# Moving part of the second step additions from VectorE to GpSimd as int32 pair sums, with a new instruction order

## The chip, the cores and the metric

The kernel runs on one core of one Trainium2 chip. The metric is the device time of one execution in microseconds. Three runs of the kernel before gave 702.07, 702.99 and 703.46 us; the median is 702.99 us.

## The reference

Two attention blocks over the same input x (2048 positions, 512 features, 32 heads of 16), mixed by a gate for each position:

```python
g = _sigmoid((x * gate_w).sum(-1, keepdims=True))
# block A: softmax attention
scores = jnp.einsum("bhqd,bhkd->bhqk", q, k) * (Dh ** -0.5)
p = _softmax(scores, axis=-1)
o = jnp.einsum("bhqk,bhkd->bhqd", p, v)
a = o.transpose(0, 2, 1, 3).reshape(B, S, D) @ wo
# block B: linear attention
phi = lambda t: jnp.where(t > 0, t + 1, jnp.exp(t)) + 1e-6
kv = jnp.einsum("bhsd,bhse->bhde", phi(k), v)
num = jnp.einsum("bhqd,bhde->bhqe", phi(q), kv)
den = jnp.einsum("bhqd,bhd->bhq", phi(q), phi(k).sum(s))[..., None] + 1e-6
b = (num / den).transpose(0, 2, 1, 3).reshape(B, S, D) @ wo_B
return g * a + (1 - g) * b
```

Nearly all the work is the exponential of the scores of block A: 32 heads x 2048 x 2048 values.

## The kernel before, in words

**Rounds and units.** The scores are made in 32 rounds. A round is four heads (every second head of a group of eight) against 512 queries, and consists of 64 units; a unit is one head's 128 keys x 512 queries, one bank of PSUM. TensorE makes the scores of a unit (`ps<-Qpad,KT`), the exponential is taken, and TensorE multiplies the result with the values (`ps<-PT,Vaug` or `ps<-DP,Vaug`) into the accumulator of the round.

**Two ways to an exponential.** ScalarE takes the units in order, two or three banks with one ACTIVATE (line 1979, output tile PT). Beside it VectorE takes units from the back of the round: a "claim". Only units from number 40 up can be claimed (`4 * KB2`), so 24 of the 64 at most. For a claimed unit VectorE reads PSUM once (line 1518) and writes an int16 number whose bits, read as float16, are a coarse exponential. Four claimed units make a bundle (`NTRI = 4`, 2048 int16 numbers a partition). Then the same bundle is written twice more with 342 and with 683 added to each number (line 1566, the step additions, z = 1 and z = 2), and TensorE multiplies all three versions with values scaled by three weights; the weighted sum smooths out the coarse exponential. So a claimed unit takes three value products, a unit of ScalarE takes one.

**The order is planned.** All instructions are laid down when the kernel is built, by a planner that keeps an estimated clock for each engine. VectorE's work waits in a list (`items`) with priorities: 0 for claims made inside a ScalarE group and for accumulator copies, 1 for other evictions and side claims, 2 for checks, 3 for step additions. `pump` takes the best item that could start. `can_claim`, `claim_in_group` and `claim_beside` decide whether a further unit goes to VectorE: they ask `dve_load`, the VectorE work that is queued, against `RING_LOAD` (claims inside a group) or `CLAIM_LOAD` (others), and whether buffers are free (13 bundles, `NB`). `claim_round` gives the round of ScalarE (`act_round`) as long as 14 of its units are left, and the next round after that. Where nothing else is due, TensorE runs multiplications of the zero tile `warm` (`fill`).

**GpSimd in the kernel before.** After the start it only makes 12 products `OT<-oraw,rbc` (line 1246), planned with `POOL_TT = 1.3` us. While such an operation runs, `est_start` lets no VectorE operation that reads only SBUF start:

```python
if E is DV and not any(res in r_bank for res in reads):
    for a, b in pool_runs:
        if a <= t < b:
            t = b
```

A path that gives step additions to GpSimd exists (`EVERY`, `POOL_ADD`) and is switched off with `EVERY = 0`; there the addition is a `tensor_scalar` over 2048 int16 numbers, planned with 2.4 us.

Of the kernel before, what the change touches and what calls it, by code (L numbers as in the profile page):

```python
# [9 lines left out]
ALU = mybir.AluOpType  # L10
# [3 lines left out]
I32 = mybir.dt.int32  # L14
I16 = mybir.dt.int16
# [15 lines left out]
STEPS = (0, 342, 683)  # L31
NG4 = len(STEPS)
# [21 lines left out]
NTRI = 4  # L54
# [150 lines left out]
def d_sb(n, rate=1.0):  # L205
    return 0.15 + n * 1.042e-3 * rate
# [6 lines left out]
def bass_gated_mix__mha_block__linear_attn_block__prompt_kernel(  # L213
# [27 lines left out]
    pairs_ = [(t8, qc) for t8 in range(NT8 - 2) for qc in range(NQC)] + LAST_ORDER  # L241
    KV0, KV1 = 1.0, 1.2
    PRE_T = 5
    PRE_GAP = 8
    OUT_GAP = 8

    with ExitStack() as es:
        _cnt = [0]

        def SB(shape, dt, name):  # L250
            _cnt[0] += 1
            return es.enter_context(nc.sbuf_tensor(f"{name}_{_cnt[0]}", list(shape), dt))
# [48 lines left out]
        NTU = 512 * NTRI  # L301

        DP = SB([128, NB, NTU], BF16, "DP")
# [5 lines left out]
        rbc = SB([128, 512], FP32, "rbc")  # L309
        dev = SB([128, 2, 128], FP32, "dev")  # L310
        flag = SB([128, 1], I32, "flag")
        epool = SB([128, 2, 512], BF16, "epool")
        KVbd = SB([128, NCC, 128], BF16, "KVbd")
        Zsel = SB([128, NCC, 8], BF16, "Zsel")
# [35 lines left out]
        PE = _Eng("pe", SEM("s_pe"), ordered=True)  # L350
# [22 lines left out]
        R = _Res  # L373
# [20 lines left out]
        r_OT = [[R(f"OT{t}_{q}") for q in range(NQC)] for t in range(NT8)]  # L394
        r_rraw = [R(f"rraw{k}") for k in range(8)]
        r_dev, r_flag = R("dev"), R("flag")
        r_e = [R("e0"), R("e1")]
        r_phiK = [[R(f"phiK{s}_{k}") for k in range(4)] for s in range(2)]
        r_phi2 = [R(f"phi2{k}") for k in range(NTB // 2)]
# [16 lines left out]
        def est_start(E, reads, writes):  # L416
            t = E.t
            for res in list(reads) + list(writes):
                if res.we is not E:
                    t = max(t, res.tw + LAT)  # L420
                elif not E.ordered:
                    t = max(t, res.tw + SELF_T)
            for res in writes:
                t = max(t, res.tr + LAT)
# [8 lines left out]
        POOL_SOON = 0.3  # L433
        POOL_TT = 1.3
        POOL_V = 0.9
        POOL_ADD = 2.4
        EVERY = 0
        OT_POOL = 1
        V2_POOL = 0

# [16 lines left out]
        def blocked(it, reads, writes):  # L457
            return blocker(it, reads, writes) is not None
# [27 lines left out]
        def settle(reads, writes):  # L486
# [31 lines left out]
        def op(E, fn, reads=(), writes=(), dur=0.2, issue=None):  # L518
            settle(reads, writes)
            return _emit(E, fn, reads, writes, dur, issue)  # L520
# [11 lines left out]
                    res.pw += 1  # L532

        WAIT_BANK = 0.12

        def pump(now, look=0.25):
            try_close()
            while items and DV.t <= now + look:
                best = None
                for it in items:  # L540
                    o = it.ops[0]
                    if len(o) > 5 or blocked(it, o[1], o[2]):
                        continue
                    st = est_start(DV, o[1], o[2])
                    wait = st - DV.t
                    key = (wait > (WAIT_BANK if it.prio <= 1 else 0.12), it.prio, st, it.seq)
                    if best is None or key < best[0]:
                        best = (key, it, st)
                if best is None:
                    return  # L550
                if best[2] > now + look + WAIT_BANK:
                    return
                emit_item_op(best[1])

        def dve_load(now):
            return max(0.0, DV.t - now) + sum(o[3] for it in items for o in it.ops)
# [135 lines left out]
                                                   pattern=pattern, channel_multiplier=mult), reads=[w], writes=[w])  # L692

        op(PO, lambda: nc.gpsimd.memset(warm[:], 0.0), writes=[r_warm])  # L694
# [758 lines left out]


        tri = [None]
        closing = [None]
        z1_out = [None, None]
        ntri = [0]

        def claim_round():  # L1460
# [13 lines left out]
        def can_claim(now, js):  # L1474

            r = claim_round()
            if r is None:
                return None
            t8, qc, half = rounds[r]
            if (t8, qc, half) not in q_done or (t8, 3) not in k_ready:  # L1480
                return None
            u = next((u for u in range(NU - 1, 4 * KB2 - 1, -1) if u >= head[r] and u % 4 in js and u not in taken[r]), None)
            if u is None:
                return None
            kt, q, rd = unit_aps(r, u)
# [3 lines left out]
            if not try_close() and (tri[0] is None or len(tri[0][1]) == NTRI - 1):  # L1489
# [7 lines left out]
        def free_buffers():  # L1497

            used = [e[3] for e in pv_pending]
            held_ = [c[0] for c in (tri[0], closing[0]) if c is not None]  # L1500
# [25 lines left out]
            pv_pending.append((r, u, [(DP[:, i, 512 * k:512 * (k + 1)].bitcast(F16), z)], r_DP[i][k], Fraction(1, NG4)))  # L1526

        def close_tri():
            if tri[0] is not None and closing[0] is None:
                closing[0] = (*tri[0], [])  # L1530
                tri[0] = None
            try_close()

        def try_close():

            while closing[0] is not None:
                i, us, zs = closing[0]
                z = len(zs) + 1
                if z == NG4:
                    closing[0] = None  # L1540
                    return True
                free = free_buffers()
                if not free:
                    return False
                i2 = free[0]
                zs.append(i2)
                n = 512 * len(us)
                y = DP[:, i, 0:n].bitcast(I16)
                mine_, out_ = r_DP[i][0:len(us)], r_DP[i2][0:len(us)]
                if EVERY and z == NG4 - 1 and n == NTU and ntri[0] % EVERY == 0:  # L1550
                    push(3, [(lambda z=z, i2=i2, y=y, n=n: nc.gpsimd.tensor_scalar(
                        DP[:, i2, 0:n].bitcast(I16), y, 1.0, float(STEPS[z]), ALU.mult, ALU.add), mine_, out_, 0.0, None, POOL_ADD)])
                    if z1_out[0] is None:
                        pool_go([])
                    else:
                        z1_out[1] = out_
                else:
                    z1_out[:] = [out_, None]

                    def added(z=z, out_=out_):  # L1560
                        if z1_out[0] is out_:
                            z1_out[0] = None
                        if z == NG4 - 1 or z1_out[1] is not None:
                            z1_out[1] = None
                            pool_go(out_)
                    push(3, [(lambda z=z, i2=i2, y=y, n=n: nc.vector.tensor_single_scalar(DP[:, i2, 0:n].bitcast(I16), y, STEPS[z], ALU.add),  # L1566
                              mine_, out_, d_sb(n, 0.25), added)])
                for k, (r, u) in enumerate(us):
# [216 lines left out]
        RES_FROM = 60  # L1785
        MARGIN = 0.15
        PV_LAG = 14
        LATE = 9
        LAG_END = 12
        A_FIRST = 200  # L1790
        LATE_END = 0
# [225 lines left out]
            g += 1  # L2017


        while tri[0] is not None or closing[0] is not None:  # L2020
            close_tri()
            if closing[0] is not None and not pv_step(PE.t, force=True):
# [242 lines left out]
```

## Time and profile before

| | |
|---|---|
| Median of 3 runs | 702.99 us |
| The profiled execution, its own time | 702.72 us |
| Its span, first to last instruction | 701.0 us |
| ScalarE busy | 687.5 us, 98% |
| TensorE busy | 676.9 us, 97% |
| VectorE busy | 660.2 us, 94% |
| GpSimd busy | 24.1 us, 3% |
| Granted TensorE clock | 1.000 of full speed |

Busy times are unions: two operations of an engine that overlap count once. A group's mean is the duration of a single operation, which is longer than the distance from one start to the next where operations of an engine overlap at their ends. A row of a list of groups names the line, the engine, the operation, output and input, the count, and behind the bar the busy time, the mean in ns and the idle time in front with what ended it.

### The profile page before, as it was taken

The numbers are of one execution on the slowest core, as the hardware profiler recorded it, in microseconds if no ns is written. First come the engines' busy times: TensorE is split into PE (matmuls) and PEld (weight loads), VectorE is DVE, ScalarE is ACT, GpSimd is POOL, SyncE is SP. The second block draws the span as 40 slices with busy tenths as digits, with TensorE's granted clock in tenths as the row PEclk, the third lists the DMA queues.
The fourth block names the chain that finished last, engine by engine and source line by source line (L and its number), as shares of the span: only waits on it lengthen the run. The fifth ranks groups of instructions, "written<-read, shape, count | busy, mean of one in ns | idle before, by whom it ended". The sixth has DMA issues, their size and how long they took to land.

```text
span 701.0 us, 19208 instructions
## 1 busy us (share of the span) xinstructions
PE 676.9 (97%) x8181; PEld 205.6 (29%) x8181; DVE 660.2 (94%) x1140; ACT 687.5 (98%) x710; POOL 24.1 (3%) x31
## 2 busy tenths in 40 slices
PE   8999999999999999999999999999999999999997
PEld 4322223332223323232322232322222222222223
DVE  4599999999999998999999999999999998999995
ACT  6999999999999999999999999999999999999996
POOL 4000000000000000000000000000000000000000
PEclk9999999999999999999999999999999999999999
DMA  9800101000010001201010011101111201010101
GB/s 222 233 2 9 25 2 34 1 14 22 10 24 2 19 16 40 50 7 33 3 22 13 14 37 17 28 15 26 31 25 29 44 13 44 17 41 18 35 23 49
DMA packets 44815, 22.96 MB, mean 33 GB/s; under 512 B 33976, under 2 KB 40568, under 8 KB 44728
## 3 DMA queue, kind: packets, MB, share of 16 engines
q1 hardware_dynamic: 42712, 20.12, 12.7%
q10 hardware_dynamic: 2016, 1.57, 0.9%
q8 instruction: 67, 1.10, 0.7%
q14 instruction: 20, 0.16, 0.1%
HBM read 8.00 MB, written 2.10 MB: 14 GB/s over the span
## 4 chain that ended last, share of the span: by engine, by line
ACT 93%; PE 6%; DVE 1%; issue 0%; POOL 0%; ACTq 0%; POOLq 0%
ACT PT L1979 90%; PE ps L646 6%; ACT epool L929 2%; DVE DP L2075 0%; DVE xT L1847 0%; PE ps L653 0%; DVE KT L818 0%; DVE DP L2080 0%; DVE flag L2085 0%; POOL warm L694 0%; POOL dummy L663 0%; ACT eg L913 0%; ACTq L2188 0%; POOLq L2250 0%
## 5 line engine op out<-in xcount | busy, mean ns | idle before, releaser
L1979 ACT ACTIVATE PT<-ps 128x1024 bf16<-128x1024 f32 (+1 forms) x670 | 679.7, 1337 | 0.6 <-PE ps L646 0.5
L1518 DVE TENSOR_SCALAR DP<-ps 128x512 int16<-128x512 f32 x584 | 384.5, 683 | 13.4 <-PE ps L646 10.5
L646 PE MATMUL ps<-Qpad,KT 32*128 32x512 bf16 x2048 | 269.1, 384 | 17.6 <-ACT PT L1979 12.8
L1566 DVE TENSOR_SCALAR DP<-DP 128x2048 int16<-128x2048 int16 x292 | 193.8, 682 | 0.0
L646 PE MATMUL ps<-DP,Vaug 128*32 128x512 f16 x1741 | 188.1, 384 | 0.3 <-DVE oraw L1258 0.3
L646 PE MATMUL ps<-PT,Vaug 128*32 128x512 bf16 x1451 | 163.5, 385 | 0.6 <-DVE Vaug L873 0.5
L646 PEld LDWEIGHTS ps<-Qpad,KT 32*128 32x128 bf16 x2048 | 67.3, 91 | 289.1 <-ACT PT L1979 265.7
L646 PE MATMUL ps<-warm 128*32 128x512 bf16 (+1 forms) x510 | 72.8, 384 | 1.1 <-POOL warm L694 1.1
L646 PEld LDWEIGHTS ps<-DP,Vaug 128*32 128x32 bf16 x1741 | 46.4, 95 | 58.5 <-issue 34.0
L646 PEld LDWEIGHTS ps<-PT,Vaug 128*32 128x32 bf16 x1451 | 38.9, 94 | 52.4 <-issue 40.6
L1246 POOL TENSOR_TENSOR OT<-oraw,rbc 128x512 bf16<-128x512 f32 x12 | 15.6, 1303 | 524.5 <-DVE DP L1566 524.5
L646 PE MATMUL ps<-xT,wA 128*32 128x512 bf16 x432 | 32.1, 384 | 0.0
L929 ACT ACTIVATE epool<-ps 128x512 bf16<-128x512 f32 x32 | 27.4, 858 | 0.0
L646 PEld LDWEIGHTS ps<-warm 128*32 128x32 bf16 (+1 forms) x510 | 18.8, 97 | 19.8 <-issue 15.2
L1258 DVE COPY oraw<-ps 128x512 f32<-128x512 f32 x31 | 21.1, 682 | 0.1
L646 PE MATMUL ps<-wB,xT 128*32 128x512 bf16 x256 | 19.3, 384 | 0.0
L646 PE MATMUL ps<-xT,wB 128*32 128x512 bf16 x256 | 18.8, 383 | 0.0
L646 PE MATMUL ps<-woA,OT 128*32 128x512 bf16 (+1 forms) x226 | 18.6, 383 | 0.0
L934 DVE SCALAR_TENSOR_TENSOR phi<-ps,epool 128x512 bf16<-128x512 f32 x24 | 16.3, 680 | 0.0
L818 DVE CAST KT<-ps 128x512 bf16<-128x512 f32 (+1 forms) x16 | 10.7, 667 | 4.9 <-PE ps L646 4.9
L646 PE MATMUL ps<-wA,xT 128*128 128x128 bf16 x192 | 14.9, 220 | 0.0
L873 DVE CAST Vaug<-ps 128x512 bf16<-128x512 f32 x16 | 10.9, 683 | 2.3 <-PE ps L646 2.3
(104 smaller groups left out, 233.1 us busy)
## 6 DMA issues: line engine op xcount, KB each, us to landing
rbc<-oraw SPq DMA_DIRECT2D x16, 256.0 KB
OT<-in_A_x_dram SPq DMA_DIRECT2D x4, 512.0 KB, 7.2
Qpad<-Qs SPq DMA_DIRECT2D x124, 16.0 KB, 1.8
oraw<-oraw SPq DMA_DIRECT2D x60, 32.0 KB, 2.0
wA<-in_A_wqkv_dram SPq DMA_DIRECT2D x1, 1536.0 KB, 7.8
wB<-in_B_wqkv_dram SPq DMA_DIRECT2D x1, 1536.0 KB, 9.0
out_dram<-outt SPq DMA_DIRECT2D x12, 128.0 KB, 1.8
phi<-in_A_x_dram ACTq DMA_DIRECT2D x3, 256.0 KB, 6.1
```

The lines of the kernel that those rows point to most:

```text
L646: return lambda: nc.tensor.matmul(o, lhsT=l, rhs=r, start=start, stop=stop, skip_group_check=sg)
L818: push(1, [(lambda: nc.vector.tensor_copy(KT[:, par, c0:c1], src), [r_bank[b]], [r_KT[par][t]], d_psum(n), None)])
L873: ops = [(lambda: nc.vector.tensor_copy(v_group(NQC * par + v)[:, :, :, 0:16], src), [r_bank[b]], [r_V[par][v]], d_psum(512), lambda: v_do ...
L929: op(AC, lambda: nc.scalar.activation(epool[:, s, :], bank_ap(b), ACT.Exp), reads=[r_bank[b]], writes=[r_e[s]], dur=0.6, issue=0.48)
L934: (lambda: nc.vector.scalar_tensor_tensor(out=dst, in0=bank_ap(b), scalar=0.0, in1=epool[:, s, :], op0=ALU.max, op1=ALU.add), [r_bank[b], ...
L1246: push(1, [(lambda: (nc.gpsimd if on_pool else nc.vector).tensor_tensor(OT[:, t8, 512 * qc:512 * (qc + 1)], oraw[:, 0, :], rbc[:], ALU.mul ...
L1258: push(0, [(lambda: nc.vector.tensor_copy(oraw[:, half, :], acc), [r_acc], [r_oraw[half]], d_psum(512), evicted)])
L1518: push(0 if in_group else 1, [(lambda: nc.vector.tensor_scalar(DP[:, i, 512 * k:512 * (k + 1)].bitcast(I16), bank_ap(b), FRAC - Y_BIAS4, Y ...
L1566: push(3, [(lambda z=z, i2=i2, y=y, n=n: nc.vector.tensor_single_scalar(DP[:, i2, 0:n].bitcast(I16), y, STEPS[z], ALU.add), mine_, out_, d ...
L1979: op(AC, lambda p0=p0, b0=b0, n=n: nc.scalar.activation(PT[:, 512 * p0:512 * p0 + n], ps[:, 512 * b0:512 * b0 + n], ACT.Exp, scale=LN2 / F ...
```

## The change

On GpSimd the second step addition (z = 2) of every second bundle is now a `tensor_tensor` addition over 1024 int32 numbers: each holds two int16 numbers, and the other operand is one int32 number a partition (683 in both halves), read again and again. It is allowed only for a full bundle whose four units are of one round, where that round is the one that ScalarE works on and not the last. `POOL_ADD`, the planned length, is 1.97 us. `pool_go` is now asked at each step of the planner; a GpSimd addition goes out behind a VectorE step addition, and if a VectorE step addition could run and none has just run, that one is first put ahead of all other VectorE work (`boost`). Closed bundles form a queue in place of a single slot, and the additions of a bundle of a later round wait while another addition is listed. Some limits of the planner have new values, and the whole order is laid down anew. The diff, cut to its core:

```diff
-    PRE_GAP = 8
+    PRE_GAP = 6
...
+        step2 = SB([128, 2], I16, "step")
...
-        POOL_ADD = 2.4
-        EVERY = 0
+        POOL_ADD = 1.97
+        EVERY = 2
+        POOL_LEFT = 22
...
-        def pool_go(sync):
+        def pool_go(sync=None):
             for it in sorted(items, key=lambda i: i.seq):
                 o = it.ops[0]
                 if len(o) > 5 and not blocked(it, o[1], o[2]) and est_start(PO, o[1], o[2]) <= DV.t + POOL_SOON:
+                    if not last_add[1] and any(x.prio == 3 and len(x.ops[0]) == 5 and not blocked(x, x.ops[0][1], x.ops[0][2])
+                                               for x in items):
+                        boost[0] = True
+                        return
+                    boost[0] = last_add[1] = False
                     STATS["pool"] = STATS.get("pool", 0) + 1
-                    emit_item_op(it, sync)
+                    emit_item_op(it, last_add[0])
                     return
...
         def pump(now, look=0.25):
             try_close()
+            pool_go()
...
-                    key = (wait > (WAIT_BANK if it.prio <= 1 else 0.12), it.prio, st, it.seq)
+                    key = (wait > (WAIT_BANK if it.prio <= 1 else 0.12), -1 if it.prio == 3 and (boost[0] or (RUSH and it.ops[0][5:] == () and due_now(it))) else it.prio, st, it.seq)
...
                 emit_item_op(best[1])
+                pool_go()
...
+        op(PO, lambda: nc.gpsimd.memset(step2[:], STEPS[2]), writes=[r_step], dur=0.1)
...
-        GATE_AT = 4.5
+        GATE_AT = 3.5
...
-        PT_URGENT = 11
+        PT_URGENT = 12
...
-            if tri[0] is None and len(free_buffers()) < CLAIM_FREE:
+            if tri[0] is None and len(free_buffers()) < (CLAIM_FREE_OPEN if closing else CLAIM_FREE):
...
+                if len(free) < (LAZY if early else 1):
+                    return False
+                if not zs and sum(1 for it in items if it.prio == 3) >= (1 if early else MOST_ADDS):
                     return False
...
-                if EVERY and z == NG4 - 1 and n == NTU and ntri[0] % EVERY == 0:
-                    push(3, [(lambda z=z, i2=i2, y=y, n=n: nc.gpsimd.tensor_scalar(
-                        DP[:, i2, 0:n].bitcast(I16), y, 1.0, float(STEPS[z]), ALU.mult, ALU.add), mine_, out_, 0.0, None, POOL_ADD)])
...
+                if (EVERY and z == NG4 - 1 and n == NTU and ntri[0] % EVERY == 0 and us[0][0] == us[-1][0] < NR - 1
+                        and us[0][0] == act_round[0] and NU - len(taken[us[0][0]]) > POOL_LEFT):
+                    push(3, [(lambda z=z, i2=i2, y=DP[:, i, 0:n].bitcast(I32), n=n: nc.gpsimd.tensor_tensor(
+                        DP[:, i2, 0:n].bitcast(I32), y, step2[:].bitcast(I32).to_broadcast([128, n // 2]), ALU.add),
+                        mine_ + [r_step], out_, 0.0, None, POOL_ADD)])
...
-        Q_OFF = 0
+        Q_OFF = -4
...
-        CLAIM_LOAD = 3.3
-        LATE_CLAIM = 4.0
-        STARVE = 7
-        MAC_LOW = 0.47
+        CLAIM_LOAD = 3.7
+        LATE_CLAIM = 4
+        STARVE = 6.0
+        MAC_LOW = 0.45
...
-        LATE = 9
+        LATE = 8
```

More of the change, by code (lines that the diff above doesn't have):

```diff
@@ L396, in bass_gated_mix__mha_block__linear_attn_block__prompt_kernel @@
         r_dev, r_flag = R("dev"), R("flag")
+        r_step = R("step")
         r_e = [R("e0"), R("e1")]
@@ L433, in bass_gated_mix__mha_block__linear_attn_block__prompt_kernel @@
         POOL_SOON = 0.3
+        POOL_PASS = 1.0
+        last_add = [[], False]
+        boost = [False]
         POOL_TT = 1.3
         POOL_V = 0.9
-        POOL_ADD = 2.4
-        EVERY = 0
+        POOL_ADD = 1.97
+        EVERY = 2
+        POOL_LEFT = 22
         OT_POOL = 1
@@ L534, in bass_gated_mix__mha_block__linear_attn_block__prompt_kernel, with due_now @@
         WAIT_BANK = 0.12
+        RUSH = 0
+        of_round = {}
+        def due_now(it):
+            return of_round.get(it.seq, NR) <= acc_round[0] < act_round[0]
         def pump(now, look=0.25):
             try_close()
+            pool_go()
             while items and DV.t <= now + look:
@@ L1455, in bass_gated_mix__mha_block__linear_attn_block__prompt_kernel @@
         tri = [None]
-        closing = [None]
-        z1_out = [None, None]
+        closing = collections.deque()
         ntri = [0]
@@ L1488, in can_claim @@
                     return None
-            if not try_close() and (tri[0] is None or len(tri[0][1]) == NTRI - 1):
+            if not try_close() and len(closing) > MOST_OPEN and (tri[0] is None or len(tri[0][1]) == NTRI - 1):
                 return None
-            if tri[0] is None and len(free_buffers()) < CLAIM_FREE:
+            if tri[0] is None and len(free_buffers()) < (CLAIM_FREE_OPEN if closing else CLAIM_FREE):
                 return None
@@ L1499, in free_buffers @@
             used = [e[3] for e in pv_pending]
-            held_ = [c[0] for c in (tri[0], closing[0]) if c is not None]
+            held_ = [c[0] for c in (tri[0], *closing) if c is not None]
             free = [i for i in range(NB) if i not in held_ and not any(x.pend or x in used for x in r_DP[i])]
@@ L1528, in close_tri @@
         def close_tri():
-            if tri[0] is not None and closing[0] is None:
-                closing[0] = (*tri[0], [])
+            if tri[0] is not None:
+                closing.append((*tri[0], []))
                 tri[0] = None
             try_close()
+        LAZY = 1
+        MOST_ADDS = 20
+        MOST_OPEN = 0
+        CLAIM_FREE_OPEN = 2
         def try_close():
-            while closing[0] is not None:
+            while closing:
                 i, us, zs = closing[0]
@@ L1539, in try_close @@
                 if z == NG4:
-                    closing[0] = None
-                    return True
+                    closing.popleft()
+                    continue
                 free = free_buffers()
-                if not free:
+                early = us[0][0] > acc_round[0]
+                if len(free) < (LAZY if early else 1):
+                    return False
+                if not zs and sum(1 for it in items if it.prio == 3) >= (1 if early else MOST_ADDS):
                     return False
@@ L1549, in try_close, with added @@
                 mine_, out_ = r_DP[i][0:len(us)], r_DP[i2][0:len(us)]
-                if EVERY and z == NG4 - 1 and n == NTU and ntri[0] % EVERY == 0:
-                    push(3, [(lambda z=z, i2=i2, y=y, n=n: nc.gpsimd.tensor_scalar(
-                        DP[:, i2, 0:n].bitcast(I16), y, 1.0, float(STEPS[z]), ALU.mult, ALU.add), mine_, out_, 0.0, None, POOL_ADD)])
[L1553 to L1556, printed above, removed]
-                else:
[L1558 to L1565, printed above, removed]
+                if (EVERY and z == NG4 - 1 and n == NTU and ntri[0] % EVERY == 0 and us[0][0] == us[-1][0] < NR - 1
[3 more added lines that the diff above has]
+                        mine_ + [r_step], out_, 0.0, None, POOL_ADD)])
+                else:
+                    def added(out_=out_):
+                        last_add[:] = [out_, True]
+                        boost[0] = False
                     push(3, [(lambda z=z, i2=i2, y=y, n=n: nc.vector.tensor_single_scalar(DP[:, i2, 0:n].bitcast(I16), y, STEPS[z], ALU.add),
                               mine_, out_, d_sb(n, 0.25), added)])
+                of_round[iseq[0]] = us[0][0]
                 for k, (r, u) in enumerate(us):
@@ L2017, in bass_gated_mix__mha_block__linear_attn_block__prompt_kernel @@
             g += 1
-        while tri[0] is not None or closing[0] is not None:
+        while tri[0] is not None or closing:
             close_tri()
-            if closing[0] is not None and not pv_step(PE.t, force=True):
+            if closing and not pv_step(PE.t, force=True):
                 flush_items()
```

## The prediction

> **What bounds the kernel now.** I read the page first: the busy times, then the chain that ended last, then the groups.
>
> ```profile
> PE 676.9 (97%) x8181; PEld 205.6 (29%) x8181; DVE 660.2 (94%) x1140; ACT 687.5 (98%) x710; POOL 24.1 (3%) x31
> ACT 93%; PE 6%; DVE 1%; issue 0%; POOL 0%; ACTq 0%; POOLq 0%
> L1979 ACT ACTIVATE PT<-ps 128x1024 bf16<-128x1024 f32 (+1 forms) x670 | 679.7, 1337 | 0.6 <-PE ps L646 0.5
> L1518 DVE TENSOR_SCALAR DP<-ps 128x512 int16<-128x512 f32 x584 | 384.5, 683 | 13.4 <-PE ps L646 10.5
> L1566 DVE TENSOR_SCALAR DP<-DP 128x2048 int16<-128x2048 int16 x292 | 193.8, 682 | 0.0
> L646 PE MATMUL ps<-DP,Vaug 128*32 128x512 f16 x1741 | 188.1, 384 | 0.3 <-DVE oraw L1258 0.3
> ```
>
> Three engines look full, but only one sets the end: the chain lies on ScalarE for 93% of the span, and its exponentials (line 1979) stood idle for 0.6 us in all. The time falls only if ScalarE gets fewer units. It made 2048 - 584 = 1464 of the 2048 units in 679.7 us, 0.464 us a unit. What it doesn't make, VectorE must claim, and 584 / 4 = 146 bundles with 292 additions show that all second additions are still on VectorE.
>
> Next, how much room the others have in the long middle, and who hides there:
>
> ```profile
> core 0: us, PE busy (x) PEld busy (x) DVE busy (x) ACT busy (x) POOL busy (x), PEclk, DMA share, GB/s
> 85.00:680.00 595.00, 579.59 (x7004) 171.24 (x7000) 579.58 (x993) 595.00 (x616) 15.64 (x12) 1.00 0.11 23
> ```
>
> From 85 to 680 us ScalarE is busy in every microsecond, VectorE is idle for 595.00 - 579.58 = 15.42 us (2.6%), TensorE for 15.41 us, and the granted clock is full. So VectorE is the second limit: it takes nearly all the claims that it can, and any time freed on it can become claims.
>
> **What an addition costs VectorE, and what a claim costs.** Two rows of the timeline with uninterrupted runs:
>
> ```profile
> 204.70 3.13 DVE L1518 TENSOR_SCALAR DP<-ps 128x512 int16<-128x512 f32 x5
> 212.01 2.49 DVE L1566 TENSOR_SCALAR DP<-DP 128x2048 int16<-128x2048 int16 x4
> ```
>
> Less one duration of 0.68 us, the distance between starts is (3.13 - 0.68) / 4 = 0.61 us for a claim's eviction and (2.49 - 0.68) / 3 = 0.60 us for a step addition. These, not the means of 683 and 682 ns, are what the engine pays.
>
> A further claim costs VectorE 0.61 us and a quarter of two additions, 0.30 us, so 0.91 us, and it takes 0.464 us from ScalarE and so from the end; VectorE then also has 0.46 us less time. Freed time of X us on VectorE therefore buys X / (0.91 + 0.46) claims, and the end moves by 0.464 / 1.37 = 0.34 X.
>
> **How many additions move.** The conditions of the diff decide. `NU - len(taken) > POOL_LEFT` always holds: at most 24 units can be claimed, and 64 - 24 = 40 is above 22. A round has 584 / 32 = 18.25 claims, and ScalarE makes 45.75 units of it. Claims go to the next round once fewer than 14 units are left, so during 13 / 45.75 = 28% of a round; these first 5.2 claims of a round are made while ScalarE is still in the round before. A bundle qualifies if its four units are of one round and its last one is claimed in that round's own time: its last unit is number 5.2 to 18.25, so (18.25 - 5.2) / 4 = 3.3 a round, 101 in the 31 rounds that are allowed, and every second one of them is about 50. All of 146 would give 73; if a bundle that waits for buffers misses its round, 30. I take 50: 50 x 0.60 = 30.0 us off VectorE (bounds 18 to 44).
>
> **What a GpSimd sum costs VectorE.** The kernel before has GpSimd operations in its middle, all waiting for a VectorE step addition like the new ones. I asked for the busy times within each of the 12, from its start to 0.1 us behind its end (first, two bad ones, sum):
>
> ```profile
> 85.37:86.74 1.37, 1.37 (x18) 0.38 (x22) 1.14 (x3) 1.37 (x3) 1.27 (x1) 1.00 0.00 0
> 331.86:333.24 1.38, 1.38 (x22) 0.56 (x20) 0.57 (x2) 1.38 (x2) 1.28 (x1) 1.00 0.08 24
> 462.03:463.41 1.38, 1.38 (x19) 0.39 (x20) 0.45 (x1) 1.38 (x3) 1.28 (x1) 1.00 0.01 0
> sum 16.84, PE 16.76 PEld 4.79 DVE 13.33 ACT 16.84 POOL 15.62; mean PE 1.40 PEld 0.40 DVE 1.11 ACT 1.40 POOL 1.30
> ```
>
> In these 16.84 us VectorE was idle for 3.51 us, 21%; outside them, in the middle, for 11.91 of 578.16 us, 2.1%. The timeline shows how:
>
> ```profile
> 462.03 1.28 POOL L1246 TENSOR_TENSOR OT<-oraw,rbc 128x512 bf16<-128x512 f32 x1 [45.28 <-DVE DP L1566]
> 461.20 0.68 DVE L1566 TENSOR_SCALAR DP<-DP 128x2048 int16<-128x2048 int16 x1
> 461.80 0.68 DVE L1518 TENSOR_SCALAR DP<-ps 128x512 int16<-128x512 f32 x1
> 463.51 0.69 DVE L1518 TENSOR_SCALAR DP<-ps 128x512 int16<-128x512 f32 x1 [1.03 <-PE ps L646]
> 464.32 0.69 DVE L1566 TENSOR_SCALAR DP<-DP 128x2048 int16<-128x2048 int16 x1
> ```
>
> The eviction runs beside GpSimd at its usual 0.68 us, then there is nothing in PSUM to read, and the next addition comes only behind the GpSimd operation, because the planner holds it back. It has reason to:
>
> ```profile
> 415.15 1.60 POOL L1246 TENSOR_TENSOR OT<-oraw,rbc 128x512 bf16<-128x512 f32 x1 [36.08 <-DVE DP L1566]
> 414.32 1.29 DVE L1566 TENSOR_SCALAR DP<-DP 128x2048 int16<-128x2048 int16 x2
> L1246 POOL TENSOR_TENSOR OT<-oraw,rbc x12: 1268/1277/1597, 85.4 to 548.4; 128x512 bf16<-128x512 f32 x12
> ```
>
> The one that started while a step addition was running (until 414.32 + 1.29 = 415.61) took 1.60 us, against a median of 1.277. The Trainium skill, SBUF — State Buffer, section "Who interferes with whom", gives this as an exclusive lock: a VectorE addition of this kind and a GpSimd instruction want the same pair of ports, the first has it for its whole length, the other is blocked. By that rule a VectorE addition that meets a GpSimd sum waits it out; this row agrees in kind, and it speaks against the change.
>
> For a sum of 1.97 us and 0.1 us behind it, the excess idle share of 21% - 2% is 0.39 us. The ends: an empty PSUM for the whole rest, at worst the 0.60 us that the addition saves; at best the six better of the twelve windows, 0.1 us. The row's 0.39 is of orders in which such operations were rare and claims stopped at a queue of 3.3 us; with `CLAIM_LOAD` at 3.7 there are 0.4 us more of evictions queued for the claims that this limit decides, so I take 0.30. Net 0.60 - 0.30 = 0.30 us for each, 50 x 0.30 = 15 us, and the end moves by 0.34 x 15 = 5.1 us, with 11 more claims.
>
> **The length of the sum.** No row has it. Two memsets give GpSimd's fixed part:
>
> ```profile
> L723 POOL MEMSET Osb<- 128x512 bf16 x1 | 0.5, 532 | 0.0
> L694 POOL MEMSET warm<- 128x128 bf16 x1 | 0.2, 205 | 0.0
> ```
>
> (532 - 205) / 384 = 0.85 ns an element and 0.10 us fixed. A product of 512 then has (1.277 - 0.10) / 512 = 2.3 ns an element, and a sum of 1024 takes 2.45 us if both operands cost as much there; at the memset's rate it would be 0.97 us. The plan's 1.97 lies between. I take it, because the plan's other GpSimd length, 1.3, agrees with the 1.277 of the trace. The Trainium skill, GPSIMD Engine Reference, section "Elementwise — side-by-side cycle accounting", has 4497 ns for a two-input addition of 2048 fp32 elements, so about 2.25 us here as an estimate from that page; by it each sum overruns its plan by 0.28 us, and less the 0.21 us of slack that the second rival below works out, 50 x 0.07 = 3.5 us would be added to the forecast.
>
> **What costs nothing.** TensorE gets two more value products a claim: 22 of 188.1 / 1741 = 0.11 us are 2.4 us, covered by its 15.41 us of idle time; without that cover they would fall on the end. The memset of the pair stands ahead of the identity in GpSimd's queue, at most the 0.2 us of the one in front; it goes if the first transposes wait for input anyway. The new limits (projections of Q four groups earlier, the gate 15 groups earlier, the last preparations closer together) move steps whose instructions stay the same:
>
> ```profile
> Qpad<-Qs SPq DMA_DIRECT2D x124, 16.0 KB, 1.8
> PEld ps L646 <- DVE DP L1518: 10.3, 43, 0.5
> ```
>
> The copies to Qpad pass the accumulator copies on SP's queue; they land 1.8 us after issue and are needed about a round (some 20 us) later. I put the new order at nothing: it can gain at most the 0.6 us that ScalarE waited, and if it doubled TensorE's waits for claims' banks (10.3 us), at 0.34, lose 3.5.
>
> **Sum.** Against the profiled execution: 702.72 - 5.1 = 697.6 us. That execution is 0.27 us under the median of the runs, so 697.9 us for a median.
>
> **The rivals.** *The cover is missing* (0.12): VectorE idles 0.5 to 0.6 us in each sum, as at 462 us, and the saved addition is given back. For it: evictions come at about one in 0.9 us, so an empty PSUM is natural. Against: only two of twelve windows were so bad. The time stays within 1.4 us of 703.0.
>
> *The sum is longer than planned* (0.18), the rival on the other side. A fixed order can't give claims back. A VectorE addition placed behind a sum is blocked for the overrun, and what stands behind it in VectorE's queue are evictions, whose banks TensorE needs for ScalarE's next scores. At 2.45 us the overrun is 0.48 us. There is one sum in 595 / 50 = 12 us, with some 10 us x 2.1% = 0.21 us of VectorE's own idle time to take it up; 50 x 0.27 = 13.5 us remain. If all of it reaches ScalarE, 711 us, if half does, 705; I put it at 708. It decides from 1.97 + 0.21 + 5.1 / 50 = 2.28 us on.
>
> *The new order feeds ScalarE worse* (0.07): ScalarE's idle time, 0.6 us now, grows by more than the 5.1 us gained, because steps and claims collide on the one spare bank; with twice the 5.1, 708. Nothing in the profile speaks for it but how tight ScalarE's feed is.
>
> *The additions hardly move* (inside the 0.12): if buffers run short and only 15 go over, the end moves by 1.5 us or less.
>
> **How the numbers follow.** What this kernel's measurement can tell from no change is about 0.2%, 1.4 us. Forecast, 0.63: 697.9. If the idle time is 0.1 us, 50 x 0.50 x 0.34 = 8.5 us, 694.5; with 73 sums 12.4 us, 690.6. The low end, 691.5, leaves out only the last of these. The high end takes in the missing cover and half of the long-sum rival, 706. Within the forecast alone: 692 to 701.5. Chances: faster 0.63, same 0.12, slower 0.18 + 0.07 = 0.25.
>
> **What would show it.** Right: some 50 GpSimd additions of about 2.0 us; the line 1566 group on VectorE down to about 250 (292 - 50 + 6); claims about 595; line 1979 busy about 675 us with idle time still near 1 us; VectorE idle within the sums near 0.4 us each. Wrong: sums of 2.3 us or more with additions of VectorE that wait behind them; ScalarE idle for several microseconds on scores; or as many claims as before, with VectorE idle in the sums.

## The result and the profile after

The changed kernel takes 697.83 us (median of 6 runs, 697.30 to 698.16) against 702.92 us (6 runs): a ratio of 0.9929, 95% interval 0.9916 to 0.9942. The gain is small and clear of the noise. The forecast was 697.9 us. The profiled execution took 698.16 us, its span is 696.4 us.

The page of the changed kernel, in the order of the lines shown of before (busy times, chain, groups; line 1999 was 1979, 1536 was 1518, 1585 was 1566):

```profile
PE 672.9 (97%) x8162; PEld 203.7 (29%) x8164; DVE 641.6 (92%) x1099; ACT 682.6 (98%) x707; POOL 139.6 (20%) x91
ACT 85%; PE 13%; DVE 0%; issue 0%; POOL 0%; ACTq 0%; POOLq 0%
L1999 ACT ACTIVATE PT<-ps 128x1024 bf16<-128x1024 f32 (+1 forms) x667 | 674.0, 1324 | 1.4 <-PE ps L664 1.3
L1536 DVE TENSOR_SCALAR DP<-ps 128x512 int16<-128x512 f32 x596 | 391.8, 683 | 24.0 <-PE ps L664 19.9
L1578 POOL TENSOR_TENSOR DP<-DP,step 128x1024 int32<-128x1024 int32 x59 | 115.2, 1952 | 438.3 <-DVE DP L1536 336.5
L1585 DVE TENSOR_SCALAR DP<-DP 128x2048 int16<-128x2048 int16 x239 | 159.3, 687 | 0.0
```

59 sums went to GpSimd, VectorE's additions fell from 292 to 239, claims rose from 584 to 596, and ScalarE's exponentials fell from 679.7 to 674.0 us with 1.4 us of idle time instead of 0.6. That is 4.9 us off ScalarE, and the span is 4.6 us shorter. But VectorE now idles 24.0 us in front of its claims, not 13.4, most of it for scores (19.9 us). The middle, 85 to 680 us (columns as in the prediction's window), says the same:

```profile
85.00:680.00 595.00, 580.79 (x7048) 170.89 (x7049) 567.04 (x964) 594.22 (x617) 122.20 (x66) 1.00 0.11 23
```

VectorE is idle for 27.96 us there; before it was 15.42. A good part of the freed time was not used.

The busy times within the 59 sums, each from its start to 0.1 us behind its end (the sum of the windows), and two GpSimd operations and the VectorE additions beside them from the timeline:

```profile
sum 120.99, PE 117.76 PEld 33.94 DVE 108.80 ACT 120.59 POOL 115.09; mean PE 2.00 PEld 0.58 DVE 1.84 ACT 2.04 POOL 1.95
```

```profile
85.91 2.27 POOL L1578 TENSOR_TENSOR DP<-DP,step 128x1024 int32<-128x1024 int32 x1 [7.07 <-DVE DP L1536]
85.75 0.68 DVE L1585 TENSOR_SCALAR DP<-DP 128x2048 int16<-128x2048 int16 x1
...
653.80 1.89 POOL L1578 TENSOR_TENSOR DP<-DP,step 128x1024 int32<-128x1024 int32 x1 [6.32 <-DVE DP L1536]
655.40 1.44 DVE L1585 TENSOR_SCALAR DP<-DP 128x2048 int16<-128x2048 int16 x2
```

VectorE idled for 120.99 - 108.80 = 12.19 us in the sums, 0.21 us each. A sum takes 1.89 us; the one at 85.91 started while a VectorE addition was running and took 0.38 us longer, and two additions that began before the one at 653.80 had ended took 1.44 instead of 1.29 us. Such meetings are few: 9 of the 59 sums took 2.27 us or more. The Trainium skill (SBUF — State Buffer, "Who interferes with whom") has the first comer hold the shared ports and the other wait, and these rows agree with it in kind, in both directions.

### The profile page after: what moved, and what is told of

Its sections match the earlier page's. It is cut to its first block, busy times and chain, and to the rows that moved or that the text cites. A ratio compares the mean times of both kernels' runs of the same rounds, so it can differ in the third digit from the quotient of the medians.

```text
span 696.4 us, 19208 instructions
## 1 busy us (share of the span) xinstructions
PE 672.9 (97%) x8162; PEld 203.7 (29%) x8164; DVE 641.6 (92%) x1099; ACT 682.6 (98%) x707; POOL 139.6 (20%) x91
## 4 chain that ended last, share of the span: by engine, by line
ACT 85%; PE 13%; DVE 0%; issue 0%; POOL 0%; ACTq 0%; POOLq 0%
ACT PT L1999 83%; PE ps L664 13%; ACT epool L948 2%; PE ps L671 0%; DVE DP L2095 0%; DVE xT L1867 0%; DVE KT L837 0%; DVE DP L2100 0%; DVE flag L2105 0%; POOL warm L712 0%; POOL dummy L681 0%; ACT eg L932 0%; POOL step L713 0%; ACTq L2208 0%; POOLq L2270 0%
## 5 line engine op out<-in xcount | busy, mean ns | idle before, releaser
L1999 ACT ACTIVATE PT<-ps 128x1024 bf16<-128x1024 f32 (+1 forms) x667 | 674.0, 1324 | 1.4 <-PE ps L664 1.3
L1536 DVE TENSOR_SCALAR DP<-ps 128x512 int16<-128x512 f32 x596 | 391.8, 683 | 24.0 <-PE ps L664 19.9
L664 PE MATMUL ps<-DP,Vaug 128*32 128x512 f16 x1779 | 203.4, 385 | 0.4 <-DVE DP L1536 0.2
L1578 POOL TENSOR_TENSOR DP<-DP,step 128x1024 int32<-128x1024 int32 x59 | 115.2, 1952 | 438.3 <-DVE DP L1536 336.5
L664 PE MATMUL ps<-PT,Vaug 128*32 128x512 bf16 x1435 | 176.8, 385 | 0.9 <-DVE oraw L1277 0.5
L1585 DVE TENSOR_SCALAR DP<-DP 128x2048 int16<-128x2048 int16 x239 | 159.3, 687 | 0.0
L664 PEld LDWEIGHTS ps<-DP,Vaug 128*32 128x32 bf16 x1779 | 48.7, 94 | 62.9 <-issue 37.6
L664 PE MATMUL ps<-warm 128*32 128x512 bf16 (+1 forms) x463 | 61.8, 385 | 1.1 <-POOL step L713 1.1
L664 PEld LDWEIGHTS ps<-PT,Vaug 128*32 128x32 bf16 x1435 | 42.5, 94 | 56.2 <-issue 44.8
L664 PEld LDWEIGHTS ps<-warm 128*32 128x32 bf16 (+1 forms) x463 | 16.1, 97 | 13.2 <-issue 9.8
```

The source lines that it names most:

```text
L664: return lambda: nc.tensor.matmul(o, lhsT=l, rhs=r, start=start, stop=stop, skip_group_check=sg)
L1536: push(0 if in_group else 1, [(lambda: nc.vector.tensor_scalar(DP[:, i, 512 * k:512 * (k + 1)].bitcast(I16), bank_ap(b), FRAC - Y_BIAS4, Y ...
L1578: push(3, [(lambda z=z, i2=i2, y=DP[:, i, 0:n].bitcast(I32), n=n: nc.gpsimd.tensor_tensor(DP[:, i2, 0:n].bitcast(I32), y, step2[:].bitcast ...
L1999: op(AC, lambda p0=p0, b0=b0, n=n: nc.scalar.activation(PT[:, 512 * p0:512 * p0 + n], ps[:, 512 * b0:512 * b0 + n], ACT.Exp, scale=LN2 / F ...
```

## Experiments

### The engine or the order?

The edits are shown abridged; `...` and `<...>` stand for code that is not printed.

Theory 1: what counts is VectorE's time. Rival: the new limits and the new order bring the gain. The first experiment keeps the changed kernel's order and lets VectorE make the 59 sums.

```diff
-            if on_pool:
+            if on_pool and on_pool[0] == POOL_ADD:
+                ev = DV.add(fn, _deps_for(reads, writes))   # planner's clocks as for GpSimd
...
-                    push(3, [(lambda ...: nc.gpsimd.tensor_tensor(... I32 ...)
+                    push(3, [(lambda ...: nc.vector.tensor_single_scalar(... I16 ..., STEPS[z], ALU.add)
```

> The changed kernel's order instruction for instruction, 596 claims, but the 59 sums are made by VectorE as step additions, each at the place in VectorE's order where the planner handed it to GpSimd. Theory 1 (what counts is VectorE's time): VectorE gets 59 x 0.60 = 35 us back; it was idle for 28 us between 85 and 680 us, but 11 of these lie in the sums and most of the rest in two starved stretches, so 10 to 24 us reach the end: 708 to 722 us, ScalarE idle for 10 us or more. Rival (the new limits and the new order bring the gain, the engine does not matter): within 1.5 us of 697.8.

Measured: 711.37 us, ratio to the kernel before 1.0121 (1.0104 to 1.0138), 13.5 us above the changed kernel. Its groups and waits:

```profile
L2010 ACT ACTIVATE PT<-ps 128x1024 bf16<-128x1024 f32 (+1 forms) x667 | 673.4, 1180 | 10.0 <-PE ps L675 8.9
PE ps L675 <- DVE DP L1547: 12.2, 29, 0.9
```

With the same 596 claims ScalarE's exponentials take about the same 673.4 us, but now ScalarE waits 10.0 us in front of them, nearly all of it for scores. The scores are late because banks are: TensorE's multiplications waited 12.2 us for claims that VectorE had not yet read out (the second row). Counted with the weight loads, the instructions for scores alone (those that read the tile KT) waited 13.1 us for them in 31 places, against 0.8 us in 2 places in the changed kernel. The chain that ended last lies on VectorE for 56% of the span. The 10.0 us are not the whole loss: ScalarE's busy time over all its lines also rose, from 682.6 to 687.6 us. So this order can't be kept up without GpSimd. The second experiment keeps everything but the sums.

```diff
-        EVERY = 2
+        EVERY = 0
```

> EVERY = 0, everything else of the change kept: the new limits, an order laid down anew with all additions on VectorE; 581 claims. Theory 1: 15 claims fewer than the changed kernel, 15 x 0.464 = 7 us more, 703 to 706 us. Rival (limits and order): 698 to 700.

Measured: 703.18 us, ratio 1.0006 (0.9996 to 1.0016). The new limits and the new queue alone bring nothing that can be measured.

```profile
L1999 ACT ACTIVATE PT<-ps 128x1024 bf16<-128x1024 f32 (+1 forms) x663 | 680.1, 1352 | 0.7 <-PE ps L664 0.5
```

### Do more sums bring more, and do the limits matter?

Three orders laid down anew: the sums with the eight moved limits at their old values, half the sums, and nearly twice the sums.

```diff
-    PRE_GAP = 6 ... GATE_AT = 3.5 ... PT_URGENT = 12 ... Q_OFF = -4 ... CLAIM_LOAD = 3.7 ... STARVE = 6.0 ... MAC_LOW = 0.45 ... LATE = 8
+    PRE_GAP = 8 ... GATE_AT = 4.5 ... PT_URGENT = 11 ... Q_OFF = 0 ... CLAIM_LOAD = 3.3 ... STARVE = 7 ... MAC_LOW = 0.47 ... LATE = 9
```

> The sums and the new queue as in the change, but the eight limits of the planner that the change moved (PRE_GAP, GATE_AT, PT_URGENT, Q_OFF, CLAIM_LOAD, STARVE, MAC_LOW, LATE) at their old values; the order laid down anew has 59 sums and 584 claims. Theory A (freed VectorE time turns into claims by itself, the limits hardly matter): 697 to 699.5 us. Theory B (the end follows the claims that the planner makes, and these depend on its limits): 12 claims fewer than the changed kernel, 12 x 0.464 = 5.6 us, 702 to 705.

```diff
-        EVERY = 2
+        EVERY = 4
```

> EVERY = 4: 29 sums in place of 59, all else as in the change; 584 claims. Theory A (in proportion to the sums): half the gain, 700.2 to 700.8 us. Theory B (by claims): 702.5 to 704.

```diff
-        EVERY = 2
+        EVERY = 1
```

> EVERY = 1: 110 sums in place of 59; 592 claims. Theory A with the prediction's 0.34 x 0.30 us a sum: 51 more sums, 5 us faster, 692 to 694. Theory B (by claims): 4 fewer, 699.5 to 700. A third case: sums so dense that VectorE's additions wait and ScalarE with them: over 701, ScalarE idle for several microseconds.

Measured: old limits 704.72 us (ratio 1.0031, 1.0019 to 1.0044), every fourth 704.49 us (1.0023, 1.0013 to 1.0032), every bundle 705.09 us (1.0027, 1.0015 to 1.0038). All three are slower than the kernel before, by more than its noise. The groups, in that order:

```profile
L1999 ACT ACTIVATE PT<-ps 128x1024 bf16<-128x1024 f32 (+1 forms) x671 | 680.2, 1317 | 2.7 <-PE ps L664 2.5
L1536 DVE TENSOR_SCALAR DP<-ps 128x512 int16<-128x512 f32 x584 | 382.9, 685 | 32.0 <-PE ps L664 28.1
```

```profile
L1999 ACT ACTIVATE PT<-ps 128x1024 bf16<-128x1024 f32 (+1 forms) x666 | 679.9, 1326 | 2.1 <-PE ps L664 1.8
L1536 DVE TENSOR_SCALAR DP<-ps 128x512 int16<-128x512 f32 x584 | 383.1, 684 | 17.4 <-PE ps L664 14.2
```

```profile
L1999 ACT ACTIVATE PT<-ps 128x1024 bf16<-128x1024 f32 (+1 forms) x685 | 677.9, 1266 | 4.1 <-PE ps L664 3.5
L1536 DVE TENSOR_SCALAR DP<-ps 128x512 int16<-128x512 f32 x592 | 390.5, 685 | 47.2 <-PE ps L664 43.6
```

Theory A falls: freed time does not become claims by itself. With the old limits the same 59 sums leave 584 claims; VectorE only waits longer for scores (32.0 us). With 110 sums it waits for 47.2 us. Theory B (the end follows the claims) holds where the claims are, and misses what comes on top: in the last case ScalarE takes longer for its units, as more of its operations hold two units instead of three (599 with two and 86 with three, not 547 and 119), and waits 4.1 us. That is the time of the third case of the expectation, but not its mechanism: VectorE's additions were not held up (689 ns in the mean, 687 in the changed kernel). In one table, with ScalarE's line as busy plus idle in front, VectorE's idle time from the window 85 to 680 us, and the runs of the next sections too:

| order | sums | claims | ScalarE, us | VectorE idle, us | median, us |
|---|---|---|---|---|---|
| before | 0 | 584 | 679.7 + 0.6 | 15.4 | 702.9 |
| no sums | 0 | 581 | 680.1 + 0.7 | 16.5 | 703.2 |
| every fourth | 29 | 584 | 679.9 + 2.1 | 30.9 | 704.5 |
| old limits | 59 | 584 | 680.2 + 2.7 | 40.0 | 704.7 |
| every bundle | 110 | 592 | 677.9 + 4.1 | 63.5 | 705.1 |
| the change | 59 | 596 | 674.0 + 1.4 | 28.0 | 697.8 |
| searched limits | 57 | 597 | 674.5 + 1.9 | 27.1 | 697.9 |
| short sum, planned | 59 | 598 | 673.3 + 1.0 | 25.2 | 698.0 |
| two products | 60 | 598 | 673.2 + 1.2 | 25.9 | 697.2 |

The median is ScalarE's column plus 21.5 to 23.7 us in every row. In part that is arithmetic, since this line and the gaps in front of it fill most of ScalarE's span; and it fails in an order that VectorE can't keep: with the sums on VectorE the difference is 711.4 - 683.4 = 28.0 us. VectorE's idle time doesn't order the rows: 16.5 us goes with 703.2, 28.0 with 697.8, 30.9 with 704.5.

### What does a sum's length cost?

The prediction's rival on the other side was a sum longer than its plan. Three kernels keep the order and put a useless GpSimd sum in front of each real one; a fourth replaces the sum by a shorter fill with zero, and so leaves the third version of these bundles out of its result.

```diff
+                    more = PO.add(lambda: nc.gpsimd.tensor_tensor(scratch[:], <256 times step2>, <256 times step2>, ALU.add),
+                        _deps_for([r_step] + sync, [r_scratch]))
                 _emit(PO, fn, reads + sync, writes, on_pool[0])
```

> The changed kernel's order, but in front of each sum GpSimd makes a second, useless sum of 256 int32 numbers, by the sum's own rate about 0.55 us, so that a sum takes about 2.44 us instead of 1.89 where the plan says 1.97. The prediction's rival on the other side: VectorE additions placed behind a sum are blocked for the overrun of 0.47 us, less 0.21 us of idle time, 59 x 0.26 = 15 us if all of it reaches ScalarE, half if half does: 705 to 713 us. Counter-theory (evictions stand behind most sums, and the idle time in the sums takes up the overrun): under 700.5 us.

Measured: 699.38 us, ratio 0.9952 (0.9935 to 0.9968), 1.5 us above the changed kernel. The experiment was weaker than meant. Of its GpSimd waits

```profile
POOL DP L1584 <- DVE DP L1542: 81.0, 30, 5.7
```

shows that 30 of the 59 real sums still waited for their units behind the useless one, which had run ahead. So it was done again with the useless sum waiting for the same things as the real one, at two lengths, 256 and 1024 numbers.

```diff
-                        _deps_for([r_step] + sync, [r_scratch]))
+                        _deps_for(reads + sync, [r_scratch]))
```

> As e2_longer_sum, whose useless sum of 0.64 us waited only for VectorE's step addition and in about half the cases ran ahead while the real sum still waited for its units; now the useless sum waits for all that the real one waits for, so that each of the 59 sums is 0.64 us longer, 2.5 us, an overrun of 0.56 us against the plan. The prediction's rival: 59 x (0.56 - 0.21) = 21 us, all or half of it: 708 to 719 us. Counter-theory (mostly evictions, which don't need the port, stand behind a sum, and an addition behind it is late without anyone waiting for it): under 702.

> The same with a useless sum of 1024 numbers: each sum takes about 3.85 us, an overrun of 1.9 us. The rival's rule (overrun less slack, all on ScalarE): 59 x 1.7 = 100 us, half of it 50: 748 to 798. Counter-theory: only the additions are late; with VectorE idle for 28 us in the middle, 0.47 us a sum, at most 59 x (1.9 - 0.47) = 84 us can reach the end, and much less does if other VectorE work stands between: 705 to 740.

Measured: 700.28 us (ratio 0.9962, 0.9948 to 0.9976) and 760.81 us (1.0858, 1.0792 to 1.0924). From the timeline of the first and of the second, a pair on GpSimd and the VectorE additions beside the second:

```profile
43.37 0.61 POOL L478 TENSOR_TENSOR scratch<-step 128x256 int32<-128x256 int32 x1 [33.75 <-DVE DP L1542]
43.94 1.89 POOL L1584 TENSOR_TENSOR DP<-DP,step 128x1024 int32<-128x1024 int32 x1
```

```profile
43.15 1.89 POOL L478 TENSOR_TENSOR scratch<-step 128x1024 int32<-128x1024 int32 x1 [33.55 <-DVE DP L1542]
45.00 1.89 POOL L1584 TENSOR_TENSOR DP<-DP,step 128x1024 int32<-128x1024 int32 x1
45.39 2.65 DVE L1591 TENSOR_SCALAR DP<-DP 128x2048 int16<-128x2048 int16 x2
```

At 43.94 + 1.89 - 43.37 = 2.46 us, just the length that the rival supposed, the cost is 2.45 us, not 10: the counter-theory holds. At 3.74 us it is 63 us, and 760.8 us lies inside the range expected by the rival (748 to 798) and above that of the counter-theory (705 to 740). But the waits are not the rival's. Two additions do take 2.65 instead of 1.29 us there; what TensorE waits for, however, is mostly the sums themselves:

```profile
PEld ps L670 <- POOL DP L1584: 50.0, 33, 2.6
PE ps L670 <- POOL DP L1584: 39.6, 31, 2.1
ACT PT L2005 <- PE ps L670: 49.5, 73, 2.1
```

In one table, with weight loads and multiplications taken together:

| TensorE's waits, us (times) | the change | sums of 2.46 us | sums of 3.74 us |
|---|---|---|---|
| value products, for a GpSimd sum | 2.0 (7) | 13.7 (29) | 89.6 (64) |
| value products, for a VectorE addition | 10.2 (37) | 13.0 (43) | 23.1 (59) |
| scores, for a claim that VectorE had not yet read out | 0.8 (2) | 1.1 (3) | 5.3 (10) |

So a late sum holds up its own value products, and what follows them in TensorE's fixed order; a late addition does the same on a smaller scale. The path of the rival, an eviction behind a blocked addition, is the last row, and stays small. These are waits and not losses. The chain that ended last lies on TensorE and on VectorE for 35% each with the longest sums, so how the 63 us divide among the paths is not shown.

The granted clock was 0.964 in the profiled execution with the 3.74 us sums (0.946 to 0.966 in its four runs) and 1.000 with those of 2.46 us; how much of the 63 us is the clock's was not separated.

```diff
-                        nc.gpsimd.tensor_tensor(DP[:, i2, 0:n].bitcast(I32), y, step2 ..., ALU.add)
+                        nc.gpsimd.memset(DP[:, i2, 0:n].bitcast(I32), 0)
```

> The changed kernel's order, but each sum is replaced by a GpSimd fill of the same 1024 int32 numbers with zero, which reads nothing and by the memsets' rate takes about 1.0 us instead of 1.89; the third version of these bundles is left out of the result. The order is fixed, so no claim is added. If what the sums cost in this order is collisions on VectorE (additions blocked behind a sum), they go: 2 us or more faster, under 696. If the plan's 1.97 us already keeps VectorE's additions out of the sums, only the few blocked ones go: 696.8 to 698.2.

Measured: 697.77 us (ratio 0.9925, 0.9909 to 0.9942), as the changed kernel. The fill takes 1.02 us in the mean, about half of a sum, and the end does not move: in this order collisions with the sums cost nothing that can be measured.

### What holds the claims back?

Two candidates for what keeps VectorE's freed time unused: its idle time within the sums, and TensorE. For the first, the short fill (the third version is left out of the result again) with a plan that knows it, in an order laid down anew:

```diff
-        POOL_ADD = 1.97
+        POOL_ADD = 1.05
```

> Each sum is replaced by the fill with zero of 0.95 us (the third version of these bundles is left out of the result), and the plan knows it: POOL_ADD = 1.05, order laid down anew, 59 fills, 598 claims. Theory A (idle time of VectorE in the sums, 12.2 us, is what it lacks for more claims): half of it goes, 0.34 x 6 = 2 us faster, 695 to 696. Rival (VectorE's time no longer limits, the end follows the claims): 2 claims, 0.9 us, and the order's own chance, 696.3 to 698.5.

Measured: 697.98 us (ratio 0.9929, 0.9912 to 0.9946). The windows of the 59 fills:

```profile
sum 69.19, PE 67.03 PEld 19.62 DVE 63.25 ACT 69.19 POOL 63.31; mean PE 1.14 PEld 0.33 DVE 1.07 ACT 1.17 POOL 1.07
```

VectorE's idle time beside GpSimd fell from 12.19 to 5.94 us, and the end did not move; the idle time in the whole middle went down by only 2.8 us. The rest turned up elsewhere. For the second, a stretch first: TensorE's busy times from 285 to 337 us, before and after.

```profile
285.00:337.00 52.00, 51.46 (x651) 15.01 (x650) 49.76 (x84) 52.00 (x53) 2.55 (x2) 1.00 0.13 28
```

```profile
285.00:337.00 52.00, 51.95 (x663) 15.40 (x663) 43.59 (x73) 52.00 (x53) 10.57 (x7) 1.00 0.11 25
```

There TensorE is full, and VectorE's idle time rose from 2.24 to 8.41 us. Leaving out one value product of each claim (the one of z = 1, so that its version is missing from the result) relieves TensorE:

```diff
-                for k, (r, u) in enumerate(us):
-                    add_products(i2, z, k, r, u)
+                if z == NG4 - 1:
+                    for k, (r, u) in enumerate(us):
+                        add_products(i2, z, k, r, u)
```

> The value product of the first step addition (z = 1) is left out, so a claim costs TensorE two products in place of three; the additions are all made. Order laid down anew, 598 claims. Theory C (in the changed kernel TensorE has become what limits, the freed VectorE time can't be used because of it): 2 us or more faster, under 696, and VectorE's idle time between 285 and 337 us, 8.4 us, falls by half. Rival (TensorE had room): 696.2 to 698.5, idle time there as it is.

Measured: 697.15 us (ratio 0.9926, 0.9910 to 0.9943).

```profile
285.00:337.00 52.00, 50.41 (x627) 14.80 (x623) 48.98 (x84) 52.00 (x55) 11.38 (x6) 1.00 0.08 18
```

The idle time in this stretch fell to 3.02 us, which speaks for TensorE as its cause there; the order was laid down anew too, so this is not shown apart from it. The end moved by 0.7 us, less than the 1.5 us between the runs of this kernel, and the claims by two: TensorE is not what holds them back elsewhere. The last run looked for a better order:

```diff
-    KV0, KV1 = 1.0, 1.2 ... MIN_LEFT = 14 ... Q_OFF = -4 ... B1 = 21 ... CLAIM_LOAD = 3.7
+    KV0, KV1 = 0.8, 1.2 ... MIN_LEFT = 12 ... Q_OFF = -6 ... B1 = 23 ... CLAIM_LOAD = 3.8
```

> The change with five limits moved again (KV1 as it was, KV0 0.8, MIN_LEFT 12, Q_OFF -6, B1 23, CLAIM_LOAD 3.8), taken from some hundred orders as the one with the earliest end by the planner's own clocks; 57 sums, 597 claims. By claims alone 697.4 us; if the planner's clocks are right in this, 2.2 us faster than the changed kernel, 695.6. Below 696.5 would say that the choice of order is worth as much as claims; 697 to 698.5 that the planner's clocks don't tell orders apart so finely.

Measured: 697.92 us (ratio 0.9925, 0.9906 to 0.9943), no better than the change. The planner's own clocks had put its end 2.2 us earlier; they don't tell orders apart so finely.

## Why the prediction was right, point by point

**ScalarE is the bound, and claims are the currency: shown for orders that the engines can keep.** In the nine orders of the table the end follows line 1999's busy and idle time; with the sums on VectorE it is VectorE that holds the end. About 595 claims and 675 us were forecast; 596 and 674.0 came.

**GpSimd's help is the cause: shown, with a condition.** In the same order without it the time is 711.4 us, without sums in an order of their own 703.2. But with the sums and the old limits it is 704.7. Neither half brings a gain alone.

**The terms of the sum were off, and their errors cancel: the number is in part luck.** The prediction had 50 sums, 0.30 us of lost VectorE time in each and a factor of 0.34. There were 59 sums. VectorE idled 0.21 us in each, or 0.16 us above the 2.1% that it idled outside GpSimd's operations before, in a window of 2.05 us. With these two numbers its own formula gives 59 x (0.60 - 0.16) x 0.34 = 8.8 us; 5.1 came.

The step that fails is "any time freed on it can become claims". VectorE's account over the whole span shows it, an estimate from the pages' busy times: 59 x 0.60 = 35.4 us left VectorE. Twelve more claims took 12 x 0.91 = 10.9 us of that, and the span is 4.6 us shorter. The other 19.9 us, 0.34 us a sum, were not used. Idle time rose by 14.0 us, from 701.0 - 660.2 = 40.8 to 696.4 - 641.6 = 54.8, and busy time fell by 5.9 us less than these counts ask for (18.6, not 24.5). Only about half of this loss lies in the sums, where the prediction put all of it. Outside them, between 85 and 680 us, VectorE idled for 16.2 of 482 us, 3.4%, where it was 2.6% over the whole middle before (GpSimd's products count in both); the prediction had nothing for that. The price of a claim was about right for the time that was used: 15.5 us for 12 claims, 1.29 us each against 1.37. But it is no exchange rate for freed time: every fourth bundle and the old limits got no claim at all for their sums.

**What costs nothing.** TensorE's extra products were said to be covered by its 15.41 us of idle time. That was a mean over the middle; from 285 to 337 us there is no cover, and VectorE lost 6 us of use there. The run with two products, in an order of its own, ended only 0.7 us earlier. The new order was put at nothing, with 3.5 us to lose: at the old limits it is 6.9 us worse with the same sums. This was the weakest step of the working. The 10.3 us from which the 3.5 were worked out are not what they were taken for: of these 43 waits 25 (6.3 us) stand before value products and only 2 (0.4 us) before scores, so they say little of how often a claim's bank is late.

**The length.** The plan's 1.97 us was right: the mean is 1.95, most sums took 1.89 and 9 took 2.27 us or more. The estimate from the Trainium skill (GPSIMD Engine Reference, "Elementwise — side-by-side cycle accounting") was 2.25 us; the measurement decides, 1.89 us for this integer sum with one repeated operand.

**The rivals.** The missing cover did not come: VectorE idled 0.21 us and not 0.5 in a sum. The long sum was priced too high: 10 us above the forecast for 2.45 us, where the run with 2.46 shows 2.45 us. The step that fails is its claim that evictions wait behind a blocked addition often enough to reach ScalarE: scores waited 1.1 us for such banks there, and 5.3 us with sums of 3.74 us. What a late sum does hold up, its own value products (13.7 and 89.6 us), the rival did not have. The worse feed did not come with the new limits (ScalarE's idle time went from 0.6 to 1.4 us).

**What stays open.** Why the planner stops near 597 claims whatever is relieved. Shorter sums, fewer products and other limits each gave 597 or 598, the change 596. That it is a rule of the planner and no engine is an inference from these, not shown. Nor was it tried which of the eight limits lets the sums pay; they were only moved together.

## What to carry to other kernels

Moving work off the second-busiest engine pays only through what the scheduler then makes of it. Count the units that changed engine in the new order before trusting any exchange rate, and lay the order for the new balance: the same offload gave 5 us or cost 2, by the planner's limits. When a forecast of a sum comes out right, check its terms one by one; here the number of sums was too low, the loss in each too high and the loss outside them missing, and the total was right.

## What the runs showed of the hardware that was not expected

A GpSimd sum of 1024 int32 numbers with one repeated operand took 1.89 us. The useless sums, both of whose operands are repeated, took 1.89 us for 1024 too; from start to start they occupied GpSimd for 43.94 - 43.37 = 0.57 us with 256 and 45.00 - 43.15 = 1.85 us with 1024, so (1.85 - 0.57) / 768 = 1.7 ns a number. The float product of two streams was estimated from its row at 2.3 ns. And the cost of a longer sum was far from proportional: 0.57 us more cost 2.45 us over 59 sums, 1.85 us more cost 63, at a lower granted clock.
